# Letting two engines read one score slot in a gated attention kernel, with a re-tuned in-kernel scheduler

## Chip, cores, metric

One core of a Trainium2 chip. The time is the device time of one execution in microseconds (us); a lower time is better. "Span" is the part of it from the first to the last instruction of the profiled execution, about 2 us less than the time. Engines: PE is TensorE's matmul side, PEld its weight load, ACT is ScalarE, DVE is VectorE, POOL is GpSimd. PSUM is the memory that matmuls write, SBUF the working memory.

## The reference, cut

```python
# x: 1 x 2048 x 512, bf16; H = 32 heads of Dh = 16; W = 8, dil = 2
def _A_ref(x, wqkv, wo):                 # full attention
    q, k, v = qkv[0], qkv[1], qkv[2]
    scores = jnp.einsum("bhqd,bhkd->bhqk", q, k) * scale
    p = _softmax(scores, axis=-1)
    o = jnp.einsum("bhqk,bhkd->bhqd", p, v)
    return (...)(o, 0, 2, 1, 3).reshape(B, S, D) @ wo

def _B_ref(x, wqkv, wo):                 # 8 earlier positions, 2 apart
    ...
    attn = _softmax(logits, axis=-1)
    o = jnp.einsum("bhsw,bhswd->bhsd", attn, vg)
    return (...) @ wo

g = _sigmoid((x * gate_w).sum(-1, keepdims=True))
return g * _A_ref(x, A_wqkv, A_wo) + (1 - g) * _B_ref(x, B_wqkv, B_wo)
```

The full attention dominates: 32 heads x 2048 x 2048 scores, in this kernel 2048 tiles of 128 keys x 512 queries. Every score needs an exponential.

## The kernel before

The kernel is a Python program that *schedules itself*: `run()` simulates PE, ACT and DVE with its own cost figures, always moves the engine that is earliest in time, and emits the next instruction for it. So a constant or a condition that is changed in one place shifts the order of all that follows.

PSUM has two score slots `s_a` (three banks and two banks), one bank `acc` for the products with v, and two `flex` banks. PE writes three or two score tiles to a slot; ACT takes the exponential of the whole slot in one instruction. DVE takes single tiles from a flex bank with an integer trick: one pass out of PSUM gives int16 bit patterns (`yb`), three shifted copies follow, and the four of them, read as fp16, are each multiplied with v. That averages the trick's error, and costs PE four products instead of one.

```python
ACT_W = (3, 2)
NYB = 5            # buffers of DVE's batches
YB_ITEMS = 2       # tiles in a batch
MISC_SLACK = 10    # a flex bank is kept for other work due within so many tiles
BACKLOG = 3.0      # us of DVE work beyond which DVE is given no tile
WARM_WIN = 3.42
WARM_BAR = 3500

def exp_dve(slot_item):                  # DVE's first pass, PSUM to int16
    (b, kt, j), bt, i, bank = slot_item
    nc.vector.tensor_scalar(out=self.yb[bt["buf"]][:, 0, i*512:(i+1)*512], in0=bank[:],
                            scalar1=A, scalar2=..., op0=ALU.mult, op1=ALU.add)

def d_wanted(now):                       # may DVE have another tile?
    if min(fx_free) > now or p >= N - 24 or p % 64 >= D_LAST:
        return False
    ...
    if any(s.acq and s.due <= p + MISC_SLACK for s in ready):
        return False
    return max(0.0, t["DVE"] - now) + sum(s.cost for s in ready if s.eng == "DVE") < BACKLOG

# PE's turn, the next slot is free: scores for the slot, one more tile for DVE
# beside a slot of three, two beside a slot of two, if a flex bank is free
for _ in range(4 - ACT_W[si]):
    if d_wanted(now):
        ev.append(d_take(ACT_W[si] + 1, [d[0] for d in ev]))
n = min(ACT_W[si], N - p)
its = items[p:p + n]
p += n
end = emit_qk(ev, [(it, self.aslot[si][:, i, :]) for i, it in enumerate(its)], now)
slot_free[si] = INF
...
# ACT's turn: the whole slot; the slot is free when ACT is done
nc.scalar.activation(out=self.pt[pi[0]][pi[1]][:, 0:n * 512],
                     in_=self.aslot[si][:, 0:n, :].rearrange("p a b -> p (a b)"),
                     func=ACT.Exp, scale=SCALE)
slot_free[si] = now + c + 0.1

# local attention: q x shifted k in halves, five buffers; two matmuls to a half
nc.vector.tensor_tensor(out=pr[m % NPR][:], in0=bq[ct][:, HS * hf:HS * hf + HS],
                        in1=bk[ct][:, o:o + HS], op=ALU.mult)
for i in range(2):
    sc = 2 * (n % 2) + i
    nc.tensor.matmul(out=self.misc[32 * sc:32 * sc + 32, :], lhsT=self.Eh[:, n // 2, :],
                     rhs=pr[m % NPR][:, i * 512:(i + 1) * 512], ..., tile_position=(0, 32 * sc))

# local attention, later: its probabilities, broadcast by DMA (erb), times v
bs.append(self.dma(bc, 7.0, deps=...))   # 7.0 us: the latency that the scheduler assumes
nc.vector.tensor_tensor(out=st_["pw"][m % 2][:], in0=st_["erb"][m % 3][:], in1=win, op=ALU.mult)
```

Of the kernel before, what the change touches and what calls it, by code (L numbers as in the profile page):

```python
# [42 lines left out]
NYB = 5  # L43
NQM = 3
YB_ITEMS = 2
MISC_SLACK = 10
PART_US = 3.0
BACKLOG = 3.0
D_LAST = 58
# [664 lines left out]
class _Fast:  # L714
# [13 lines left out]
    def setup(self):  # L728
# [15 lines left out]
        self.oT = [c([P, S], BF16, name=f"oT{i}") for i in range(4)]  # L744
# [17 lines left out]
        self.flex = [p([P, 512], F32, name=f"flex{i}") for i in range(2)]  # L762
# [34 lines left out]
        ei = self.wk.tile([P, 16, 32], I32, name="ei", tag="t1")[:, 0:4, :]  # L797
        ef = self.wk.tile([P, 16, 32], F32, name="ef", tag="t1")[:, 0:4, :]
# [120 lines left out]
    def jobs(self):  # L919
# [75 lines left out]
        def gate_t():  # L995
            nc.vector.tensor_scalar(out=self.eg[:], in0=self.eg[:], scalar1=1e18, scalar2=None, op0=ALU.min)
            te = self.wk.tile([P, 16, 32], F32, name="t1", tag="t1")
            nc.vector.transpose(out=te[:].rearrange("p a b -> p (a b)"), in_=self.eg[:])
            gs = self.wk.tile([P, 16], F32, name="gs", tag="gs")
            nc.vector.tensor_scalar(out=gs[:], in0=te[:, :, 0], scalar1=1.0, scalar2=None, op0=ALU.add)  # L1000
            nc.vector.reciprocal(out=gs[:], in_=gs[:])
            for qc in range(NQC):
                for j in range(4):
                    nc.sync.dma_start(out=self.gA[32 * j:32 * j + 32, qc, :], in_=gs[32 * qc:32 * qc + 32, :])
# [8 lines left out]
    def jobs_b(self):  # L1013
# [4 lines left out]
        def b1_open():  # L1018
# [6 lines left out]
            for i in range(5):  # L1025
                pr[i] = BP["1"].tile([P, S // 2], BF16, name=f"prod{i}")
# [25 lines left out]
        NPR = len(range(5))  # L1052
        HS = S // 2
        for w in range(WIN):
            pd = []
            for n in range(8):
                m = 8 * w + n

                def prod(ct=n // 2, hf=n % 2, w=w, m=m):
                    o = PAD - DIL * w + HS * hf  # L1060
                    nc.vector.tensor_tensor(out=pr[m % NPR][:], in0=bq[ct][:, HS * hf:HS * hf + HS],  # L1061
                                            in1=bk[ct][:, o:o + HS], op=ALU.mult)
                s = Step("DVE", T_D2(HS), prod, deps=allp, rel=R1 + R1w * w + 5 * n, due=R1 + R1w * w + 60, cls=3)
                self.steps.append(s)
                pd.append(s)

            def lg(n, m):
                for i in range(2):
                    sc = 2 * (n % 2) + i
                    nc.tensor.matmul(out=self.misc[32 * sc:32 * sc + 32, :], lhsT=self.Eh[:, n // 2, :],  # L1070
                                     rhs=pr[m % NPR][:, i * 512:(i + 1) * 512], start=(n < 2), stop=(n >= 6),
                                     tile_position=(0, 32 * sc))

            def ex(w=w):
                nc.scalar.activation(out=self.er[:, w, :], in_=self.misc[:], func=ACT.Exp, scale=SCALE)  # L1075
                if w:
                    nc.gpsimd.memset(self.er[0:32, w, 0:DIL * w], 0.0)
            ch = self.chain([("PE", MM, lambda n=n, w=w: lg(n, 8 * w + n)) for n in range(8)] +
                            [("ACT", T_ACT(512), ex)], due=R1 + R1w * w + 70, deps=pd[:NPR])
            for n in range(8):  # L1080
                ch[n].deps.append(pd[n])
                m = 8 * w + n
                lgs.append(ch[n])
                if m >= NPR:
                    pd[n].deps.append(lgs[m - NPR])
                    if n >= NPR:
                        pd[n].cls = 0
# [9 lines left out]
        def den_ev():  # L1097
# [4 lines left out]
            st_["erb"] = [b2([P, 4, 512], BF16, name=f"erb{i}") for i in range(3)]  # L1102
# [9 lines left out]
        prev = den = ch[-1]  # L1112
# [27 lines left out]
        for sc in range(4):  # L1140
            for ct in range(4):
# [3 lines left out]
                for hf in range(2):  # L1145
                    m = 2 * i + hf

                    def bc(sc=sc, ct=ct, m=m, hf=hf):
                        for hl in range(8):
                            p = 32 * sc + 8 * ct + hl  # L1150
                            nc.sync.dma_start(  # L1151
                                out=st_["erb"][m % 3][16 * hl:16 * hl + 16, :, :].rearrange("p w s -> p (w s)"),
# [15 lines left out]
                for hf in range(2):  # L1168
                    m = 2 * i + hf

                    def prod(i=i, hf=hf, m=m):
# [3 lines left out]
                        nc.vector.tensor_tensor(out=st_["pw"][m % 2][:], in0=st_["erb"][m % 3][:], in1=win,  # L1175
# [22 lines left out]
        self.check_flag(self.guard + [den])  # L1198
# [87 lines left out]
    def run(self):  # L1286
        nc = self.nc
        NB = 32
        items = [(b, kt, j) for b in range(NB) for kt in range(NKT) for j in range(4)]
# [7 lines left out]
        slot_free = [SLOT_0] * na  # L1297
        nextslot = 0
# [10 lines left out]
        fx_free = [1.5, DVE_0]  # L1309
# [35 lines left out]
        def exp_dve(slot_item):  # L1345
            (b, kt, j), bt, i, bank = slot_item
            A = SCALE * math.log2(math.e) * 1024.0
            nc.vector.tensor_scalar(out=self.yb[bt["buf"]][:, 0, i * 512:(i + 1) * 512], in0=bank[:],  # L1348
                                    scalar1=A, scalar2=1024.0 * (15.0 + PW_S[0]), op0=ALU.mult, op1=ALU.add)

# [6 lines left out]
        def close_batch():  # L1357
# [4 lines left out]
            prev = bt["p1"][-1]  # L1362
            lasts = []
            for k in range(1, NP_):
                s = Step("DVE", T_D4(n), lambda k=k: piece(bt, k), deps=list(bt["p1"]), due=bt["due"], cls=2)
                self.steps.append(s)
                lasts.append(s)

            def done(end):
                for i, it in enumerate(bt["items"]):  # L1370
                    rhs = [self.yb[bt["buf"]][:, k, i * 512:(i + 1) * 512].bitcast(F16) for k in range(NP_)]
                    add_pv(it, rhs, end, ("y", bt))
                bt["refs"] = len(bt["items"])
            lasts[-1].on_done = done

        def add_pv(it, rhs, ready, src):
# [5 lines left out]
            q.insert(i, [b, kt, rhs, ready, src])  # L1382

        def emit_pv_one(j, now):
            b, kt, rhs, ready, src = pvq[j][0]
# [4 lines left out]
            r = rhs.pop(0)  # L1390
            last = False
            if not rhs:
                pvq[j].pop(0)
                jleft[(b, j)] -= 1
                last = jleft[(b, j)] == 0
                left[b] -= 1
                kind, ref = src
                if kind == "p":
                    pt_refs[ref] -= 1
                    if pt_refs[ref] == 0:  # L1400
                        pt_free[ref] = now + 0.45
                else:
                    ref["refs"] -= 1
                    if ref["refs"] == 0:
                        yb_free[ref["buf"]] = now + 0.45
# [8 lines left out]
        def norm_steps(b, now):  # L1414
# [3 lines left out]
            def n1():  # L1418
                h["t1"] = self.wk.tile([P, 16, 32], F32, name="t1", tag="t1")
                nc.vector.transpose(out=h["t1"][:].rearrange("p a b -> p (a b)"), in_=self.acc[:])  # L1420

            def n2():
                rc = self.wk.tile([P, 16], F32, name="rc", tag="rc")
                nc.vector.reciprocal(out=rc[:], in_=h["t1"][:, :, DH])
                nc.vector.tensor_tensor(out=rc[:], in0=rc[:], in1=self.gA[:, qc, :], op=ALU.mult)
                nc.vector.tensor_tensor(out=self.t2[(b // 2) % 2][:, :, 16 * par:16 * par + 16], in0=h["t1"][:, :, 0:DH],
                                        in1=rc[:].unsqueeze(2).to_broadcast([P, 16, DH]), op=ALU.mult)
# [7 lines left out]
            s2 = Step("DVE", 0.75, n2, deps=[s1, self.gate_done], due=64 * b + 40, cls=2)  # L1435
            self.steps += [s1, s2]
            if par == 1:
                s3 = Step("DVE", 0.62, n3, deps=[s2], due=64 * b + 40, cls=2)
# [21 lines left out]
        def take_step(s, eng, now):  # L1460
            if s.acq:
                s.chain["i"] = min(range(2), key=lambda i: fx_free[i])
# [27 lines left out]
        def d_wanted(now):  # L1490
            if min(fx_free) > now or p >= N - 24 or p % 64 >= D_LAST:
                return False
            if batch is None and min(yb_free) > now:
                return False
            ready = [s for s in self.steps if s.rel <= p and s.eng in ("PE", "DVE") and ready_time(s) <= now + 1.5]
            if any(s.acq and s.due <= p + MISC_SLACK for s in ready):
                return False
            return max(0.0, t["DVE"] - now) + sum(s.cost for s in ready if s.eng == "DVE") < BACKLOG

        def d_take(reach, taken):  # L1500
            nonlocal p, batch
            b = items[p][0]
            js = [it[2] for it in taken]
            win = [i for i in range(p, min(p + reach, 64 * (b + 1))) if items[i][2] not in js]
            x = min(win, key=lambda i: (dcount.get((b, items[i][2]), 0), i))
            it = items.pop(x)
            items.insert(p, it)
            p += 1
# [9 lines left out]
            fi = min(range(2), key=lambda i: fx_free[i])  # L1518
            fx_free[fi] = INF
            bank = self.flex[fi]  # L1520
            d0 = Step("X", 0, None)
            s = Step("DVE", T_D1(512), lambda: exp_dve((it, bt, n, bank)), deps=[d0], due=0, cls=1)

            def p1done(end):
                fx_free[fi] = end
# [8 lines left out]
        def emit_qk(dv, ac, now):  # L1534
            nonlocal mode
            for it, dst in [d[:2] for d in dv] + ac:
                b, kt, j = it
                ct, qc, par = geo(b)
                nc.tensor.matmul(out=dst, lhsT=self.kT[ct % 2][32 * j:32 * j + 32, kt * 128:(kt + 1) * 128],  # L1539
                                 rhs=self.qm[(4 * ct + qc) % NQM][par][32 * j:32 * j + 32, :],  # L1540
                                 start=True, stop=True, tile_position=(32 * j, 0))
            did_work(now, 128 * (len(dv) + len(ac)))
# [9 lines left out]
        while True:  # L1552
# [19 lines left out]
            if eng == "ACT":  # L1572
# [7 lines left out]
                elif aq:  # L1580
# [3 lines left out]
                    if start <= now:  # L1584
                        aq.pop(0)
                        n = len(its)
                        nc.scalar.activation(out=self.pt[pi[0]][pi[1]][:, 0:n * 512],  # L1587
# [152 lines left out]
```

## Time and profile before

| before | value | from |
|---|---|---|
| time, median of the first 5 runs | 797.59 us | the times |
| time, median of all 15 runs beside the changed kernel | 798.31 us (796.36 to 799.72) | the times |

Two more views are needed. First the groups by form for DVE and for the local attention's matmuls. The columns are line, engine, operation, out<-in, shapes, count, then busy us and mean ns of one, then idle time of the engine just before them and what ended it.

```profile
L1348 DVE TENSOR_SCALAR yb<-flex 128x512 int16<-128x512 f32 x371 | 246.3, 681 | 35.2 <-PE s_a L1539 27.5 <-PE flex L1539 6.6
...
L1354 DVE TENSOR_SCALAR yb<-yb 128x1024 int16<-128x1024 int16 x537 | 199.4, 418 | 1.3
...
L1354 DVE TENSOR_SCALAR yb<-yb 128x512 int16<-128x512 int16 x39 | 9.0, 286 | 0.0
...
L1070 PE MATMUL flex<-prod,Eh 128*32 128x512 bf16 x128 | 24.7, 387 | 0.1
```

Second, the one hole in the middle, in the timeline of all engines (start, duration, instruction, count; in brackets the idle time before it and what ended that).

```profile
476.05 1.23 DVE L1175 TENSOR_TENSOR pw<-erb,vc 128x2048 bf16<-128x2048 bf16 x1 [2.31 <-DMA erb<-er_dram]
477.19 0.71 DVE L1420 STREAM_TRANSPOSE t<-acc 128x512 f32<-128x512 f32 x1
...
477.96 0.62 PE L1407 MATMUL acc<-pt,vaug 128*32 128x512 bf16 x4 [2.34 <-DVE t L1420]
...
478.51 0.61 PE L1539 MATMUL s_a<-qm,kT 32*128 32x512 bf16 x2
...
479.15 1.02 ACT L1587 ACTIVATE pt<-s_a 128x1024 bf16<-128x1024 f32 x1 [2.27 <-PE s_a L1539]
```

Read it from the top: DVE stands 2.31 us before a DMA. Behind that product waits a transpose that clears `acc`, so PE stands 2.34 us; behind PE's products wait the next scores; so ACT stands 2.27 us. One late transfer passes through three engines, each of which does its work in order.

### The profile page before, as it was taken

The numbers are of one execution on the slowest core, as the hardware profiler recorded it, in microseconds if no ns is written. First come the engines' busy times: TensorE is split into PE (matmuls) and PEld (weight loads), VectorE is DVE, ScalarE is ACT, GpSimd is POOL, SyncE is SP. The second block draws the span as 40 slices with busy tenths as digits, with TensorE's granted clock in tenths as the row PEclk, the third lists the DMA queues.
The fourth block names the chain that finished last, engine by engine and source line by source line (L and its number), as shares of the span: only waits on it lengthen the run. The fifth ranks groups of instructions, "written<-read, shape, count | busy, mean of one in ns | idle before, by whom it ended". The sixth has DMA issues, their size and how long they took to land.

```text
span 797.9 us, 20303 instructions
## 1 busy us (share of the span) xinstructions
PE 735.4 (92%) x8438; PEld 241.9 (30%) x8438; DVE 684.9 (86%) x1447; ACT 767.7 (96%) x686; POOL 6.1 (1%) x25
## 2 busy tenths in 40 slices
PE   8999999999999888999988989989998999999995
PEld 4333333333322222222322222223322322332232
DVE  5789999896789999999999966998999988877861
ACT  4899999999999999999999998999999999999994
POOL 1000000000000000000000000000000000000000
PEclk9999999999999999999999998999999999999999
DMA  5110000000000000000000345312222221000001
GB/s 152 56 29 15 8 8 9 8 2 8 15 8 1 9 1 1 2 2 2 1 2 1 116 124 138 89 56 53 74 54 60 71 51 48 15 22 15 15 14 32
DMA packets 26070, 27.65 MB, mean 35 GB/s; under 512 B 16881, under 2 KB 21489, under 8 KB 25841
## 3 DMA queue, kind: packets, MB, share of 16 engines
q1 hardware_dynamic: 25120, 24.70, 11.5%
q8 instruction: 68, 1.11, 0.6%
q0 software_dynamic: 288, 1.05, 0.4%
q10 hardware_dynamic: 560, 0.52, 0.2%
q14 instruction: 34, 0.27, 0.1%
HBM read 23.07 MB, written 3.15 MB: 33 GB/s over the span
## 4 chain that ended last, share of the span: by engine, by line
ACT 53%; issue 18%; PE 18%; DVE 6%; SPq 3%; DMA 0%; DVEq 0%; ACTq 0%
ACT pt L1587 53%; PE acc L1407 5%; PE flex L823 5%; PE s_a L1539 4%; SPq L1151 3%; DVE yb L1348 2%; PE flex L1539 2%; DVE yb L1354 1%; DVE prod L1061 1%; ACT er L1075 1%; PE s_a L860 0%; DVE pw L1175 0%; PE s_a L823 0%; PE flex L887 0%; PE flex L1070 0%
## 5 line engine op out<-in xcount | busy, mean ns | idle before, releaser
L1587 ACT ACTIVATE pt<-s_a 128x1536 bf16<-128x1536 f32 (+1 forms) x671 | 761.9, 1365 | 11.9 <-PE s_a L1539 10.5
L1539 PE MATMUL s_a<-qm,kT 32*128 32x512 bf16 x1677 | 264.4, 384 | 44.3 <-ACT pt L1587 40.7
L1348 DVE TENSOR_SCALAR yb<-flex 128x512 int16<-128x512 f32 x371 | 246.3, 681 | 35.2 <-PE s_a L1539 27.5
L1407 PE MATMUL acc<-pt,vaug 128*32 128x512 bf16 x1677 | 254.0, 387 | 3.2 <-DVE t L1420 3.2
L1407 PE MATMUL acc<-yb,vaug 128*32 128x512 f16 x1484 | 212.6, 384 | 0.0
L1354 DVE TENSOR_SCALAR yb<-yb 128x1024 int16<-128x1024 int16 (+1 forms) x576 | 207.6, 409 | 1.3
L1539 PEld LDWEIGHTS <-kT 32*128 32x128 bf16 x2048 | 93.8, 91 | 322.6 <-issue 316.5
L1539 PE MATMUL flex<-qm,kT 32*128 32x512 bf16 x371 | 125.5, 383 | 2.7 <-DVE yb L1348 1.5
L1407 PEld LDWEIGHTS <-vaug 128*32 128x32 bf16 x3161 | 85.4, 95 | 134.6 <-issue 95.5
L823 PE MATMUL flex<-xT,ww 128*32 128x512 bf16 x1280 | 103.1, 384 | 2.0 <-DVE xT L866 0.5
L1175 DVE TENSOR_TENSOR pw<-erb,vc 128x2048 bf16<-128x2048 bf16 x32 | 39.0, 1219 | 8.7 <-DMA erb<-er_dram 7.5
L1061 DVE TENSOR_TENSOR prod<-bq,bk 128x1024 bf16<-128x1024 bf16 x64 | 42.0, 682 | 2.2 <-PE flex L1070 2.1
L823 PE MATMUL flex<-pw,ident 128*32 128x512 bf16 x512 | 42.0, 394 | 0.3 <-DVE yb L1348 0.2
L823 PEld LDWEIGHTS <-ww 128*32 128x32 bf16 x1280 | 26.7, 95 | 34.6 <-issue 26.4
L1420 DVE STREAM_TRANSPOSE t<-acc 128x512 f32<-128x512 f32 x32 | 22.6, 706 | 11.9 <-PE acc L1407 11.9
L1070 PE MATMUL flex<-prod,Eh 128*32 128x512 bf16 x128 | 24.7, 387 | 0.1
L849 DVE TENSOR_SCALAR qm<-flex,pmask 128x512 bf16<-128x512 f32 x31 | 22.7, 740 | 1.7 <-PE flex L823 1.7
L853 DVE TENSOR_REDUCE amx<-flex 128x1 f32<-128x512 f32 x32 | 21.8, 681 | 0.0
L1332 PE MATMUL acc<-wz 128*32 128x512 bf16 x160 | 20.5, 382 | 0.0
L823 PE MATMUL flex<-wAv,xT 128*32 128x128 bf16 (+1 forms) x512 | 18.3, 274 | 0.4 <-DVE vaug L842 0.4
L1190 DVE CAST oB<-flex 128x512 bf16<-128x512 f32 x16 | 11.0, 686 | 8.4 <-PE flex L823 8.4
L823 PE MATMUL flex<-woB,oB 128*32 128x512 bf16 x224 | 17.2, 382 | 0.0
(90 smaller groups left out, 231.9 us busy)
## 6 DMA issues: line engine op xcount, KB each, us to landing
erb<-er_dram SPq DMA_DIRECT2D x256, 64.0 KB, 2.3
out_dram<-ob SPq DMA_DIRECT2D x14, 128.0 KB, 1.7
x_in<-in_A_x_dram SPq DMA_DIRECT2D x3, 512.0 KB, 6.3
ww<-in_B_wqkv_dram SPq DMA_DIRECT2D x12, 128.0 KB, 2.5
ww<-in_A_wqkv_dram SPq DMA_DIRECT2D x8, 128.0 KB, 2.7
er_dram<-er SPq DMA_DIRECT2D x1, 1024.0 KB, 5.1
woA<-in_A_wo_dram POOLq DMA_DIRECT2D x1, 512.0 KB, 4.3
woB<-in_B_wo_dram POOLq DMA_DIRECT2D x1, 512.0 KB, 5.0
```

What stands on the lines that cost most here:

```text
L823: self.nc.tensor.matmul(out=out_ps[32 * c:32 * c + 32, 0:n], lhsT=lhsT_of(c), rhs=rhs, start=start, stop=stop, tile_position=(0, 32 * c))
L849: self.nc.vector.tensor_scalar(out=self.qm[(4 * ct + sc) % NQM][par][:], in0=self.misc[:], scalar1=self.pmask[:, par:par + 1], scalar2=Non ...
L1061: nc.vector.tensor_tensor(out=pr[m % NPR][:], in0=bq[ct][:, HS * hf:HS * hf + HS], in1=bk[ct][:, o:o + HS], op=ALU.mult)
L1070: nc.tensor.matmul(out=self.misc[32 * sc:32 * sc + 32, :], lhsT=self.Eh[:, n // 2, :], rhs=pr[m % NPR][:, i * 512:(i + 1) * 512], start=(n ...
L1151: nc.sync.dma_start(out=st_["erb"][m % 3][16 * hl:16 * hl + 16, :, :].rearrange("p w s -> p (w s)"), in_=st_["er_d"][p:p + 1, 2048 * hf:20 ...
L1175: nc.vector.tensor_tensor(out=st_["pw"][m % 2][:], in0=st_["erb"][m % 3][:], in1=win, op=ALU.mult)
L1348: nc.vector.tensor_scalar(out=self.yb[bt["buf"]][:, 0, i * 512:(i + 1) * 512], in0=bank[:], scalar1=A, scalar2=1024.0 * (15.0 + PW_S[0]), ...
L1354: nc.vector.tensor_scalar(out=y[:, k, 0:n], in0=y[:, 0, 0:n], scalar1=float(round(1024.0 * (PW_S[k] - PW_S[0]))), scalar2=None, op0=ALU.add)
L1407: nc.tensor.matmul(out=self.acc[32 * j:32 * j + 32, :], lhsT=v, rhs=r, start=first, stop=last, tile_position=(0, 32 * j))
L1420: nc.vector.transpose(out=h["t1"][:].rearrange("p a b -> p (a b)"), in_=self.acc[:])
L1539: nc.tensor.matmul(out=dst, lhsT=self.kT[ct % 2][32 * j:32 * j + 32, kt * 128:(kt + 1) * 128], rhs=self.qm[(4 * ct + qc) % NQM][par][32 * ...
L1587: nc.scalar.activation(out=self.pt[pi[0]][pi[1]][:, 0:n * 512], in_=self.aslot[si][:, 0:n, :].rearrange("p a b -> p (a b)"), func=ACT.Exp, ...
```

## The change

The intent: give DVE more tiles without more flex banks. When a full slot of three is about to be filled and DVE has less than `BACKLOG_S` of work, DVE takes the third tile *in the slot itself*, and ACT's instruction covers two banks instead of three. The two readers are declared independent of one another ("readers of different banks"); the next scores for the slot wait for both. To make room on DVE: batches of four tiles instead of two (fewer, wider copies), local products in whole tiles, normalisation for two heads at once. Space for that comes from laying two of the three `erb` tiles into `er`. Products with v are now released copy by copy, not after the last copy.

```diff
-NYB = 5
+NYB = 3
-YB_ITEMS = 2
-MISC_SLACK = 10
+NFLEX = 2
+YB_ITEMS = 4
+MISC_SLACK = 0
 BACKLOG = 3.0
+BACKLOG_S = 1.5
+SLOT_D = 3
@@ the scores of a slot @@
-                    its = items[p:p + n]
-                    p += n
-                    end = emit_qk(ev, [(it, self.aslot[si][:, i, :]) for i, it in enumerate(its)], now)
+                    slot_users[si] = 1
+                    slot_end[si] = 0.0
+                    if not ev and n == ACT_W[si] and n >= SLOT_D and (p + n - 1) // 64 == p // 64 and d_wanted(now, False):
+                        it = d_pick(n, [])
+                        items.insert(p + n - 1, it)
+                        n -= 1
+                        its = items[p:p + n]
+                        p += n + 1
+                        slot_users[si] = 2
+                        ev.append(d_add(it, self.aslot[si][:, n, :], lambda end, si=si: slot_done(si, end)))
+                    else:
+                        its = items[p:p + n]
+                        p += n
+                    end = emit_qk(ev, [(it, self.aslot[si][:, i, :]) for i, it in enumerate(its)], now,
+                                  si=si, share=slot_users[si] == 2)
@@ waits @@
+        def decouple(r):
+            ...
+            self.tc.declare_no_dep(a, d, reason="readers of different banks")
+            self.tc.declare_no_dep(d, a, reason="readers of different banks")
+            (DVE waits for its own score matmul, ACT for the two others)
+                if prev is not None and prev.get("share") and (share or it not in [d[0] for d in dv]):
+                    for k in ("act", "dve"):
+                        self.tc.add_manual_dep(raw(q), raw(prev[k]).name, info, reason="slot free")
@@ local attention @@
-            for i in range(5):
-                pr[i] = BP["1"].tile([P, S // 2], BF16, name=f"prod{i}")
+            for i in range(2):
+                pr[i] = BP["1"].tile([P, S], BF16, name=f"prod{i}")
+                for sc in range(4):
+                    nc.tensor.matmul(out=self.misc[32 * sc:32 * sc + 32, :], lhsT=self.Eh[:, ct, :],
+                                     rhs=pr[m % 2][:, sc * 512:(sc + 1) * 512], ..., tile_position=(0, 32 * sc))
-            st_["erb"] = [b2([P, 4, 512], BF16, name=f"erb{i}") for i in range(3)]
+            st_["erb"] = [self.er[:, 0:4, :], self.er[:, 4:8, :], b2([P, 4, 512], BF16, name="erb")[:]]
@@ cut: products released copy by copy, normalisation of two heads together, moved buffers @@
```

## The prediction

> **What bounds the kernel now.** I read the busy shares first, then the slices, then ScalarE's instruction forms, then who waits for whom, then stretches of time.
>
> ```profile
> PE 735.4 (92%) x8438; PEld 241.9 (30%) x8438; DVE 684.9 (86%) x1447; ACT 767.7 (96%) x686; POOL 6.1 (1%) x25
> ...
> DVE  5789999896789999999999966998999988877861
> ACT  4899999999999999999999998999999999999994
> ```
>
> ACT is busy 96% of 797.9 us, and its idle time sits in the first and last slice. PE (92%) and DVE (86%) are not far behind: whoever relieves ACT has little room elsewhere. The work is 2048 score tiles of 128x512 whose exponential is needed. ACT takes most of them, three or two to an instruction; DVE takes the rest by an integer trick (one pass out of PSUM, then three shifted copies, so four products with v instead of one).
>
> ```profile
> L1587 ACT ACTIVATE pt<-s_a 128x1536 bf16<-128x1536 f32 x335 | 527.5, 1575 | 4.9 <-PE s_a L1539 3.9 <-PE acc L1407 0.9
> L1587 ACT ACTIVATE pt<-s_a 128x1024 bf16<-128x1024 f32 x336 | 388.2, 1156 | 7.0 <-PE s_a L1539 6.6 <-PE acc L1407 0.2
> ```
>
> The groups of instructions by form, ACT alone. 335x3 + 336x2 = 1677 tiles, so DVE has 371. One more tile in an instruction costs 1575 - 1156 = 419 ns. Neighbours overlap: the page's union of both groups is 761.9 us (671 instructions), so beside the tiles each instruction costs (761.9 - 1677 x 0.419) / 671 = 0.088 us. ACT's idle before them is only 11.9 us.
>
> ```profile
> PE s_a L1539 <- ACT pt L1587: 40.7, 115, 1.0
> ACT pt L1587 <- PE s_a L1539: 10.5, 7, 4.4
> DVE pw L1175 <- DMA erb<-er_dram: 7.5, 5, 2.5
> ```
>
> The waits: PE waits for ACT to free a score slot 115 times, 40.7 us in all; the other way it is 7 times. So the path is ACT, not PE. Hence one tile taken from ACT is worth about 0.419 us of the end, as long as PE and DVE keep up.
>
> ```profile
> core 0: us, PE busy (x) PEld busy (x) DVE busy (x) ACT busy (x) POOL busy (x), PEclk, DMA share, GB/s
> 240.00:300.00 60.00, 53.01 (x508) 16.70 (x504) 59.22 (x128) 60.00 (x56) 0.09 (x1) 1.00 0.02 4
> 420.00:480.00 60.00, 53.60 (x542) 16.48 (x538) 51.00 (x103) 57.73 (x52) 0.00 (x0) 0.97 0.28 83
> 480.00:540.00 60.00, 55.23 (x638) 16.75 (x630) 51.13 (x103) 57.60 (x52) 0.00 (x0) 0.97 0.34 94
> 600.00:660.00 60.00, 55.90 (x629) 18.08 (x627) 55.64 (x125) 60.00 (x54) 0.00 (x0) 1.00 0.23 58
> ```
>
> The stretches: ACT is full (60.00 of 60) even where DVE is full too (59.22). The one hole in the middle is around 480 us, 2.3 + 2.4 us of ACT, with the granted clock at 0.97: there DVE stands before a broadcast DMA, PE behind DVE, ACT behind PE.
>
> **What the Trainium skill says.** "PSUM — Partial Sum Buffer", Specifications (TRN2): ScalarE and VectorE read PSUM side by side at full rate as long as they do not collide in a bank. The change lives on this: ACT and DVE will read different banks of one slot. The trace before agrees so far: DVE's 128x512 read of a flex bank takes 681 ns while ACT reads nearly always. "VectorE: DVE Perf Modes", The perf-mode tier table: a tensor_scalar on 16-bit SBUF data runs at 4x, 693 ns for 2048 elements. The trace has 418 ns for 1024 and 286 for 512, thus 132 ns per 512 and, extended, 682 for 2048: it agrees. "TensorE: Matmul & The Clock Gate", Part 1: after an idle window of some 3.4 us the array runs at half clock. The trace agrees: after DVE's stall near 477 us the groups of four matmuls come 0.43 us apart and not 0.22.
>
> **The change part by part.** A scheduler inside the kernel decides the order, so I counted instructions in the built program.
>
> (1) *ACT.* DVE may now take the third tile of a three-tile slot; that happens 64 times. Other settings change too, so the built program has 275 ACT instructions of 1536 and 404 of 1024: 825 + 808 = 1633 tiles, 44 fewer, in 679 instructions, 8 more. Cost: 1633 x 0.419 + 679 x 0.088 = 744.0 against 761.9: **-17.9 us**, on the path. By stages, in blocks of 64 tiles as DVE's order has them: DVE gets +19 tiles in the first nine blocks, +6 in the next eight, +12 and +7 after; so the gain is spread, and smallest where DVE was full.
>
> (2) *Start.* ACT stands for about 4.4 us near 22 us until the second chunk of keys exists. Two of the 44 tiles come off before that, and there ACT would only wait longer: **+0.8 us**.
>
> (3) *DVE.* First passes 415 instead of 371 at 246.3/371 = 0.664: +29.2. Copies: now mostly four tiles wide; 207.6 us before are 1113 tile-widths x 0.132 plus 576 x 0.105; after, 1245 widths and 348 instructions give 164.3 + 36.5 = 200.8: -6.8. The 64 half products (42.0) become 32 whole ones of the shape of pw (39.0 for 32): -3.0. Normalisation done for two heads at once: 26.8 us of small operations become about 18.6: -8.2. Sum +11 us: 696 of some 780, 89%. Off the path, but no longer with much room.
>
> (4) *PE.* Four products instead of one for each moved tile: +176 acc matmuls from DVE's tiles, -44 from ACT's, -16 fillers. They run four at a time in different column groups; counted so, the built program has 916 groups into acc against 918, so they fill gaps in groups. Score rounds rise from 693 to 717: 24 x about 0.32 us (score matmul to next matmul in the timeline) = +8 us. PE waits 40.7 us for ACT today, so it fits, with less left.
>
> (5) *Coupling.* After a shared round the next scores in that slot wait for ACT and DVE both. In the built program neither reader waits for the other of the same round. DVE's read needs 0.68 us plus its queue (the scheduler allows 1.5 us of backlog). ACT needs the slot back after its other slot (0.93) and this one (0.93), and has a further 0.93 before it starves, less about 0.5 for the scores. So DVE is late only now and then. I put 64 x 0.05 = **+3 us**, chosen, not derived.
>
> (6) *The stage near 480 us.* The broadcast tiles now lie in er's own space, still three buffers, same DMAs. But the first pw products stand among more exponentials: in DVE's order, the first eight span 47 rows instead of 27. They ask the DMAs for less at once. Of ACT's 4.7 us lost there, and some 2 us elsewhere, I take **-4 us**; new waits of this kind, from a schedule that differs everywhere, I put at **+1 us**.
>
> Sum: 797.6 - 17.9 + 0.8 + 3 - 4 + 1 = 780.5; the end-to-end cadence of full ACT stretches (about 1.34 and 0.92 us) makes (1) 18.2, and I round down to **780**.
>
> **The rivals.** *A: the wait moves to DVE.* DVE is in order, runs about 9% longer than the scheduler's own cost figures (0.664 against 0.608 for a first pass), and now holds a slot that ACT needs. If each of the 64 shared rounds loses 0.3 us, 19 us go and the time is about 797. For it: DVE is at 95 to 99% from 240 to 420 us. Against: only 9 of the 64 shared rounds stand in those blocks, and before the change PE hardly ever waits for DVE's first pass (1.5 us in all) though it already shares flex banks with it. *B: PE becomes the bound*, with more score rounds, fewer fillers and shorter ACT rounds; a cold stretch of 3.4 us costs ACT about a microsecond or two. Five more of them would give 787. For it: 92% busy. Against: the 40.7 us of waiting for ACT. *C: the DMA hole near 480 us and the other middle waits vanish wholly* and the coupling costs nothing: 797.6 - 17.1 - 6.5 = 774.
>
> **Range and chances.** The ACT term is counted and sure to about 1 us; what is open is ACT's lost time in the middle, 6 to 7 us today, which may become 1 (774) or 13 (787). The middle is 780, and the line for 2% is near 781.8, so it is close: predicted **780.0**, range **773.0 to 787.0**, faster by over 2% **0.6**, within 2% **0.39**, slower **0.01**.
>
> **What would show each step right or wrong.** ACT's exponentials: 679, union near 744 us, means still 1575 and 1156 (a longer mean says that two readers of one slot disturb each other, and that the skill's sentence does not hold). DVE first passes on s_a: 64 at 681 ns. DVE busy 690 to 705, PE 740 to 748. "PE s_a waits for DVE yb" in the waits: under 5 us if (5) holds, over 15 if rival A does; it would stand beside new ACT waits for PE. Near 480 us ACT idle under 3 us if (6) holds. PE's wait for ACT shrinks from 40.7 to some 25 to 35. The prediction is wrong if ACT's idle before its exponentials rises above 18 us (from 11.9), or if the clock falls in more stretches than now.

## The result, and the profile after

| | before | after |
|---|---|---|
| time, median (range, runs) | 798.31 us (796.36 to 799.72, 15) | 779.5 us (776.23 to 783.34, 8) |
| ratio, 95% interval | | 0.9762 [0.9744, 0.9781] |
| tiles by ACT / DVE (of these in a shared slot) | 1677 / 371 (0) | 1633 / 415 (64) |
| union of ACT's exponentials | 761.9 us | 743.7 us |
| ACT idle just before them | 11.9 us | 7.6 us |
| PE busy / DVE busy | 735.4 / 684.9 us | 723.7 / 702.0 us |

A ratio is the mean time of one kernel's fast runs over that of the other's in the same rounds, so it is not quite the ratio of the medians quoted. The result is faster, by 18.8 us in the medians.

The two *profiled* executions differ by more, 23.0 us of span (797.9 to 774.9): that of before was 2.0 us over its median (in time), with a mean granted clock of 0.989, and that of after 2.7 us under, with 0.998. The ten executions of the changed kernel whose clock is known go from 774.4 us of span at 0.997 to 781.5 at 0.986, some 0.6 us for each 0.001 of clock. What follows about the traces concerns these two executions.

Busy shares and slices of the changed kernel:

```profile
PE 723.7 (93%) x8554; PEld 232.4 (30%) x8554; DVE 702.0 (91%) x1186; ACT 749.6 (97%) x694; POOL 5.5 (1%) x25
...
DVE  5998999989899999999999999999999998878971
ACT  4999999999999999999999999999999999999994
```

ACT has no slice below 9 between the first and the last, and DVE's dent of two sixes is gone. Groups by form, ACT, then DVE, then the local matmuls:

```profile
L1654 ACT ACTIVATE pt<-s_a 128x1024 bf16<-128x1024 f32 x404 | 435.0, 1141 | 5.3 <-PE s_a L1597 5.2
...
L1654 ACT ACTIVATE pt<-s_a 128x1536 bf16<-128x1536 f32 x275 | 431.1, 1568 | 2.3 <-PE s_a L1597 1.3 <-PE acc L1432 0.8
...
L1351 DVE TENSOR_SCALAR yb<-flex 128x512 int16<-128x512 f32 x351 | 232.7, 681 | 26.1 <-PE s_a L1597 17.4 <-PE flex L1597 7.3
...
L1375 DVE TENSOR_SCALAR yb<-yb 128x2048 int16<-128x2048 int16 x273 | 178.2, 683 | 0.6
...
L1351 DVE TENSOR_SCALAR yb<-s_a 128x512 int16<-128x512 f32 x64 | 43.8, 684 | 6.2 <-PE s_a L1597 5.8
...
L1071 PE MATMUL flex<-prod,Eh 128*32 128x512 bf16 x128 | 14.1, 384 | 0.0
```

Sixty three-tile instructions have become 68 two-tile ones. DVE's read of a bank in a shared slot takes 684 ns, of a flex bank 681. If ACT's instructions are paired with DVE's reads round by round, the two reads overlap in time in 62 of the 64 rounds, and ACT's two-tile instructions still follow one another at 917 ns, as in the trace before. So the two readers do not disturb each other. The same 128 local matmuls now fill 14.1 us and not 24.7. The waits (who waits for whom; us in all, times, longest):

```profile
PE s_a L1597 <- ACT pt L1654: 34.5, 103, 1.0
...
PEld L1597 <- ACT pt L1654: 21.7, 47, 0.8
...
ACT pt L1654 <- PE s_a L1597: 6.5, 5, 4.8
...
PEld L1597 <- DVE yb L1351: 0.4, 1, 0.4
```

PE still waits for ACT, ACT for PE only five times, of which one is the start (4.8 us). The wait that the change could have brought, scores of a slot waiting for DVE, was seen once, 0.4 us. Part of it could hide where ACT released later than DVE; then it cost nothing: in the same pairing DVE was done with its bank before ACT in 58 of the 64 rounds, and over 0.5 us later in three. The stretches, in the columns of the stretch view shown in the prediction:

```profile
240.00:300.00 60.00, 54.67 (x541) 17.12 (x543) 59.40 (x90) 60.00 (x57) 0.58 (x3) 1.00 0.01 4
420.00:480.00 60.00, 57.39 (x641) 17.59 (x640) 58.11 (x99) 59.49 (x56) 0.00 (x0) 1.00 0.36 98
480.00:540.00 60.00, 57.76 (x696) 17.42 (x694) 55.00 (x95) 59.70 (x57) 0.00 (x0) 1.00 0.23 63
600.00:660.00 60.00, 57.82 (x706) 17.50 (x703) 53.49 (x99) 59.63 (x56) 0.00 (x0) 1.00 0.25 61
```

From 420 to 540 us ACT's idle time is 0.5 + 0.3 = 0.8 us; it was 2.3 + 2.4 = 4.7.

So the 23.0 us between the traces are: ACT's exponentials 18.2, ACT's idle time before them 4.3, the rest 0.5.

### The profile page after: what moved, and what is told of

The parts are those of the page before. It is cut to its first block, busy times and chain, and to the rows that moved or that the text cites.

```text
span 774.9 us, 20388 instructions
## 1 busy us (share of the span) xinstructions
PE 723.7 (93%) x8554; PEld 232.4 (30%) x8554; DVE 702.0 (91%) x1186; ACT 749.6 (97%) x694; POOL 5.5 (1%) x25
## 4 chain that ended last, share of the span: by engine, by line
ACT 58%; PE 20%; issue 19%; DVE 2%; ACTq 0%; DVEq 0%
ACT pt L1654 57%; PE flex L827 6%; PE acc L1432 5%; PE s_a L1597 5%; PE flex L1597 2%; ACT er L1076 1%; PE s_a L864 0%; PE s_a L827 0%; DVE yb L1351 0%; PE flex L891 0%; DVE prod L1063 0%; PE s_a L868 0%; DVE ob L1265 0%; DVE vaug L846 0%; PE acc L1335 0%
## 5 line engine op out<-in xcount | busy, mean ns | idle before, releaser
L1654 ACT ACTIVATE pt<-s_a 128x1024 bf16<-128x1024 f32 (+1 forms) x679 | 743.7, 1314 | 7.6 <-PE s_a L1597 6.5
L1597 PE MATMUL s_a<-qm,kT 32*128 32x512 bf16 x1697 | 265.9, 382 | 39.2 <-ACT pt L1654 34.5
L1351 DVE TENSOR_SCALAR yb<-flex 128x512 int16<-128x512 f32 x351 | 232.7, 681 | 26.1 <-PE s_a L1597 17.4
L1432 PE MATMUL acc<-yb,vaug 128*32 128x512 f16 x1660 | 238.7, 383 | 0.0
L1375 DVE TENSOR_SCALAR yb<-yb 128x2048 int16<-128x2048 int16 (+3 forms) x348 | 204.9, 627 | 0.7
L1597 PE MATMUL flex<-qm,kT 32*128 32x512 bf16 x351 | 120.8, 383 | 1.5 <-DVE vaug L846 0.3
L1432 PEld LDWEIGHTS <-vaug 128*32 128x32 bf16 x3293 | 78.0, 95 | 129.9 <-issue 102.0
L1351 DVE TENSOR_SCALAR yb<-s_a 128x512 int16<-128x512 f32 x64 | 43.8, 684 | 6.2 <-PE s_a L1597 5.8
L1063 DVE TENSOR_TENSOR prod<-bq,bk 128x2048 bf16<-128x2048 bf16 x32 | 38.3, 1217 | 0.2 <-PE flex L1071 0.2
L1444 DVE STREAM_TRANSPOSE t<-acc 128x512 f32<-128x512 f32 x32 | 22.7, 708 | 11.8 <-PE acc L1432 11.6
L1175 DVE TENSOR_TENSOR pw<-er,vc 128x2048 bf16<-128x2048 bf16 x22 | 26.8, 1218 | 0.4 <-issue 0.4
L857 DVE TENSOR_REDUCE amx<-flex 128x1 f32<-128x512 f32 x32 | 21.7, 681 | 0.0
L1335 PE MATMUL acc<-wz 128*32 128x512 bf16 x144 | 17.9, 381 | 0.0
L827 PE MATMUL flex<-woA,oT 128*32 128x512 bf16 x224 | 17.0, 384 | 0.0
```

What stands on the lines that cost most here:

```text
L827: self.nc.tensor.matmul(out=out_ps[32 * c:32 * c + 32, 0:n], lhsT=lhsT_of(c), rhs=rhs, start=start, stop=stop, tile_position=(0, 32 * c))
L857: self.nc.vector.tensor_reduce(out=self.amx[:, row, ct, sc:sc + 1], in_=self.misc[:], axis=AX.X, op=ALU.max, apply_absolute_value=True)
L1063: nc.vector.tensor_tensor(out=pr[m % 2][:], in0=bq[ct][:], in1=bk[ct][:, o:o + S], op=ALU.mult)
L1335: nc.tensor.matmul(out=self.acc[32 * j:32 * j + 32, :], lhsT=self.wz[:, 0:32], rhs=self.wz[:], start=False, stop=False, tile_position=(0, ...
L1351: ins = nc.vector.tensor_scalar(out=self.yb[bt["buf"]][:, 0, i * 512:(i + 1) * 512], in0=bank[:], scalar1=A, scalar2=1024.0 * (15.0 + PW_S ...
L1375: nc.vector.tensor_scalar(out=y[:, k, 0:n], in0=y[:, 0, 0:n], scalar1=float(round(1024.0 * (PW_S[k] - PW_S[0]))), scalar2=None, op0=ALU.add)
```

## The experiments

All twelve gave correct results. The table has them all; "ACT work" is the prediction's count, 0.419 us per tile and 0.088 per instruction. ACT idle and PE's wait for DVE's first pass are from the profiled execution. The runs were taken in sets on different chips; the kernel before, run beside each set, had medians of 797.3 to 799.5 us, so the ratio is the fairer comparison between sets.

| run | tiles shared | DVE tiles | ACT work | time, median us (runs) | ratio to before [95%] | ACT idle | PE waits for first pass |
|---|---|---|---|---|---|---|---|
| before | 0 | 371 | 761.7 | 798.31 (15) | 1 | 11.9 | 1.7 |
| after | 64 | 415 | 744.0 | 779.5 (8) | 0.9762 [0.9744, 0.9781] | 7.6 | 0.7 |
| e1_noshare | 0 | 384 | 755.8 | 796.57 (12) | 0.9968 [0.9941, 0.9995] | 10.4 | 2.6 |
| e2_backlog_s3 | 154 | 446 | 733.1 | 792.52 (4) | 0.9917 [0.9884, 0.9949] | 26.3 | 8.0 |
| e3_slot2 | 123 | 449 | 730.6 | 786.55 (4) | 0.9860 [0.9821, 0.9899] | 23.8 | 5.9 |
| e4_before_dma11 | 0 | 373 | 760.8 | 793.96 (4) | 0.9932 [0.9911, 0.9952] | 7.5 | 2.0 |
| e5_noshare_dma11 | 0 | 376 | 759.4 | 790.49 (20) | 0.9924 [0.9903, 0.9944] | 10.4 | 3.1 |
| e6_batches_of_two | 48 | 404 | 748.4 | 788.19 (4) | 0.9895 [0.9838, 0.9953] | 10.7 | 3.1 |
| e7_backlog_s2 | 101 | 428 | 739.4 | 781.35 (4) | 0.9804 [0.9776, 0.9832] | 15.5 | 4.4 |
| e8_dma11_backlog4 | 71 | 427 | 738.8 | 780.76 (4) | 0.9782 [0.9752, 0.9812] | 14.4 | 2.2 |
| e9_longer_hold_shared | 64 | 415 | 744.0 | 804.13 (17) | 1.0068 [1.0049, 1.0087] | 26.9 | 18.5 |
| e10_same_load_on_flex | 64 | 415 | 744.0 | 797.43 (20) | 0.9986 [0.9973, 0.9999] | 22.1 | 21.9 |
| e11_more_fillers | 76 | 425 | 739.9 | 777.69 (4) | 0.9738 [0.9706, 0.9770] | 10.5 | 2.2 |
| e12_misc_slack_10 | 96 | 419 | 743.3 | 782.85 (5) | 0.9794 [0.9771, 0.9816] | 13.0 | 5.4 |

**e1_noshare: the change without the sharing.**

```diff
-SLOT_D = 3
+SLOT_D = 4
```

> The changed kernel with the sharing of a three-tile slot switched off (a slot must have 4 tiles before DVE may take one, and none has). All else of the change stays. In the built program ACT has 1664 tiles in 666 instructions, so 1664 x 0.419 + 666 x 0.088 = 755.8 us of exponentials against 744.0. Theory (ACT is the path, a tile is worth 0.419 us): 779.5 + 11.8 = 791 us, ACT idle before its exponentials near that of the changed kernel (7.6 us). Rival (the gain comes from the wider batches, the finer product order and the missing hole near 480 us, and sharing only trades one wait for another): 783 us or less.

Measured: ratio 0.9968, median 796.57 against the 791 that I expected. Two things were missed. The hole is still there, and larger. Its stretches (same columns):

```profile
420.00:480.00 60.00, 55.52 (x567) 16.92 (x566) 51.19 (x85) 55.30 (x49) 0.00 (x0) 0.97 0.29 89
480.00:540.00 60.00, 53.09 (x621) 16.79 (x622) 51.84 (x85) 58.89 (x54) 0.00 (x0) 1.00 0.37 96
```

ACT loses 4.7 + 1.1 us there, and DVE's products again wait for the broadcast DMAs. And the mean clock of its twelve runs was 0.987 against 0.9935 for the changed kernel. So everything in the diff except the sharing is worth 2 to 3 us here; the sharing makes the other 16.4 (0.0206 of 798). The difference in ACT work is only 755.8 - 744.0 = 11.8; the rest goes with the hole and the clock, which this run does not tell apart.

**e2_backlog_s3, e7_backlog_s2 and e3_slot2: more sharing.**

```diff
-BACKLOG_S = 1.5
+BACKLOG_S = 3.0    # e2;  2.0 in e7
```
```diff
-SLOT_D = 3
+SLOT_D = 2         # e3: also the second tile of the two-bank slot
```

> The changed kernel with the backlog that DVE may have when it takes a tile out of a shared slot raised from 1.5 to 3.0 us: 154 shared rounds instead of 64, DVE 446 tiles instead of 415, ACT work 733.1 us instead of 744.0. Theory while ACT stays the path and the slot comes back in time: 779.5 - 10.9 = 768.6 us. Rival A (DVE holds the slot): DVE gets 31 tiles x about 1.15 us = 36 us more, 738 us busy, and the slot waits for it; waits of PE for DVE yb above 10 us and a time of 776 us or more.

> Between the change (backlog 1.5 us, 64 shared rounds, 779.5 us) and backlog 3.0 us (154 rounds, 792.5 us): backlog 2.0 us, 101 rounds, ACT work 739.4 us. If ACT alone were the path: 779.5 - 4.6 = 775 us. From the other two runs: with 154 rounds ACT's idle before its exponentials was about 25 us instead of 7.6, which is 0.2 us per extra round; so 37 more rounds cost about 7 us and give back the 4.6: 781 to 783 us. Waits of PE for DVE's first pass between the 0.4 us of the change and the 7.8 us of backlog 3.0.

> The changed kernel with sharing allowed in the two-tile slot as well: 70 + 53 shared rounds, DVE 449 tiles, ACT work 730.6 us in 689 instructions. Theory while ACT stays the path: 779.5 - 13.4 = 766 us. Rival A: DVE about 39 us busier (741 us), and a two-tile slot whose ACT part takes only about 0.5 us comes back late; then 774 us or more with new ACT waits for PE behind DVE.

Measured: each takes more from ACT and none is faster; e2 and e3 are clearly slower than the change, e7 came as forecast (781 to 783), but its interval overlaps the change's. ACT work 744.0, 739.4, 733.1 for thresholds of 1.5, 2.0, 3.0 us; ACT idle 7.6, 15.5, 26.3; time 779.5, 781.4, 792.5. The waits of e2:

```profile
ACT pt L1654 <- PE s_a L1597: 16.5, 28, 4.0
...
ACT pt L1654 <- PE acc L1432: 8.6, 7, 2.2
...
PEld L1597 <- DVE yb L1351: 4.6, 11, 0.8
...
PE s_a L1597 <- DVE yb L1351: 1.9, 5, 0.7
```

At 3.0 us something like rival A appears: PE waits for DVE's first pass 8.0 us (under the 10 that the forecast named), and ACT waits for PE's scores 28 times where it had been five. What costs most here is not told apart. DVE is also busy 29.7 us more (731.7 against 702.0); at the 0.4 us per us that e10 below measures, this alone would be an estimated 12 of the 24 us lost (13.0 in the medians and 10.9 of ACT work saved). So the threshold keeps the change clear of a loss, but whether the held slot or DVE's load makes it is open.

e3 shows another limit. Its groups by form:

```profile
L1654 ACT ACTIVATE pt<-s_a 128x1536 bf16<-128x1536 f32 x274 | 412.9, 1507 | 11.3 <-PE s_a L1597 8.2 <-PE acc L1432 1.8
...
L1654 ACT ACTIVATE pt<-s_a 128x512 bf16<-128x512 f32 x53 | 34.3, 648 | 5.7 <-PE s_a L1597 5.7
```

In that trace one tile takes ACT 0.49 us end to end, and of the 53 instructions that follow such a one, 49 end at least 0.16 us later than the full cadence allows: 18 of them by 0.16 to 0.18 us, the others by up to 0.97; the median of all is 0.28. In the 0.49 us the *other* slot must be refilled, and it is not. So I estimate the round trip of a slot, from ACT's end through the score matmuls to ACT's next instruction, at 0.49 + 0.16 = 0.65 us or more; an ACT instruction shorter than that starves the next one. The sharing of the change leaves 0.92 us (two tiles), which is long enough.

**e4_before_dma11 and e5_noshare_dma11: the hole by itself.** The scheduler's assumed latency of the broadcast DMA, in the kernel before (e4) and in the change without sharing (e5):

```diff
-                    bs.append(self.dma(bc, 7.0, ...
+                    bs.append(self.dma(bc, 11.0, ...
```

> The kernel before with one number of its scheduler changed: the latency it assumes for a broadcast of er from 7 to 11 us, so that it spreads the first pw products (order in DVE: first eight over 75 rows instead of 27). ACT work 760.8 against 761.7 us, thus nearly unchanged. Theory (the hole near 480 us is DVE before a DMA, PE behind DVE, ACT behind PE): the ACT idle of 4.7 us between 420 and 540 us falls under 1.5 us and the time by 3 to 5 us, ratio about 0.995. Rival (the hole is due to something else in that stage, as flex banks or the cold clock alone): time within 1 us of the kernel before, hole still there.

> The changed kernel without sharing, and with the broadcast latency that the scheduler assumes at 11 us instead of 7. Without sharing alone the time was 796.6 us and ACT stood 6.2 us between 474 and 492 us. ACT work is 759.4 us, 3.6 more than without sharing alone. Theory (the hole is one cause and the tiles are the other): hole under 1.5 us, time 796.6 + 3.6 - 5.5 = about 794 us, and its runs closer together than the 792 to 803 us of the one with the hole. Rival (the loss without sharing has another source than the broadcasts): 797 us or more, hole still there.

Measured: e4 has ratio 0.9932, median 793.96, as expected. Its stretches:

```profile
420.00:480.00 60.00, 54.96 (x541) 17.01 (x536) 56.83 (x120) 60.00 (x54) 0.00 (x0) 1.00 0.26 76
480.00:540.00 60.00, 57.63 (x669) 17.98 (x668) 48.93 (x95) 59.90 (x54) 0.00 (x0) 1.00 0.31 86
```

ACT is full in both, and DVE's wait for the broadcast falls from 7.5 to 0.2 us:

```profile
DVE pw L1175 <- PE flex L823: 8.3, 6, 2.4
...
DVE pw L1175 <- DMA erb<-er_dram: 0.2, 1, 0.2
```

DVE now waits for PE instead (8.3 us, before: 0.8), and ACT does not feel it. So one constant in the old kernel is worth about 5.4 us (0.0068 of 798), with no sharing. e5 has ratio 0.9924, 790.49, better than the expected 794. Fifteen of its twenty runs have a span of 786.4 to 789.3 at a clock of 0.994 or more, five have 793.5 to 796.9 at 0.980 to 0.985; the profile fell on one of the five. With the hole treated, the change without sharing is thus no better than the old kernel with the hole treated. Against e5, the sharing is worth 0.0162 of 798, 12.9 us, for 15.4 us of ACT work.

**e6_batches_of_two: the change with the old batches.**

```diff
-NYB = 3
-YB_ITEMS = 4
+NYB = 5
+YB_ITEMS = 2
```

> The changed kernel, sharing on, with DVE's batches as before: two tiles in five buffers instead of four in three. The 348 copies become 636 narrower ones, which cost about 19 us more of DVE by 132 ns per 512 plus 105 ns each for the same tiles; the scheduler then gives DVE 404 tiles instead of 415, 48 shared. ACT work 748.4 us. Theory: only the work counts, 779.5 + 4.4 = 784 us. Rival (wider batches were the main thing of the change): 790 us or more.

Measured: 788.19, interval 0.9838 to 0.9953: inconclusive between the two forecasts. Two of its runs have spans of 782 and 783 us at clock 0.997, two have 790 at 0.984. At like clock it is thus about 7 us slower than the change (774.4 to 775.6 at 0.995 to 0.998), of which 748.4 - 744.0 = 4.4 is ACT work: DVE, busy 709.9 us, gets 11 tiles fewer. That points to wide batches as what pays for part of the sharing, but on four runs only.

**e8_dma11_backlog4: can the idle time that is left be won?**

```diff
-BACKLOG = 3.0
+BACKLOG = 4.0
@@ and the assumed latency 7.0 -> 11.0, as in e5 @@
```

> An attempt at a better version: the change, with the broadcast latency assumed at 11 us, and the backlog for tiles that go through a flex bank (not a shared slot) at 4.0 instead of 3.0 us. DVE 427 tiles, 71 of them shared, ACT work 738.8 us, 5.2 less than the change. Theory (a flex bank holds up no slot of ACT's, so longer DVE queues are cheap there): 779.5 - 5.2 = 774 us. Rival (DVE, at 91%, is full, and the longer queue makes PE wait for copies): 779 us or more, with new waits of PE acc for DVE yb.

Measured: 780.76, no better than the change; the expected 774 was missed. ACT work fell by 5.2 us, to 738.8, ACT's idle time rose by 6.8, to 14.4. In this order ACT stands 1.4 + 4.7 us in the two stretches from 420 to 540 us, some of it behind PE's products into `acc` (1.85 and 1.35 us) with hardly any wait of DVE for a DMA (0.9 us there). The hole is thus not cured by any one constant: where the local attention's products meet the score rounds, each order has its own waits.

**e9_longer_hold_shared and e10_same_load_on_flex: what a longer hold of a slot costs.** Both add 64 useless DVE operations of 0.68 us (128x512, f32), in an otherwise unchanged order. In e9 each stands just before a first pass on a shared slot, so that the slot is held so much longer; in e10 each stands before every fifth first pass on a flex bank, the same load elsewhere.

```diff
+            if id(bt["items"][i]) in self.shared:                     # e9
+            if id(bt["items"][i]) not in self.shared: (every fifth)   # e10
+                z = self.wz[:].bitcast(F32).unsqueeze(1).to_broadcast([P, 2, 256])
+                nc.vector.tensor_tensor(out=self.dum[:]..., in0=z, in1=z, op=ALU.mult)
```

> The changed kernel, instruction for instruction, plus one useless VectorE operation of about 0.69 us (a 128x512 float product of zeros into a tile that nobody reads) just before each of the 64 reads of a shared slot: DVE gets 44 us more and holds each shared slot 0.69 us longer. Theory (DVE is off the path, slots come back in time with little to spare): a part of the 64 x 0.69 is absorbed; +5 to +20 us, seen as waits of PE for DVE's first pass on s_a. Rival A as it was put (the wait has already moved to DVE in the changed kernel): the whole 44 us, about 823 us.

> The control: the same 64 useless operations, before every fifth read of a flex bank and not of a shared slot. DVE gets the same 44 us. If only the holding of a slot costs, this stays within 5 us of 779.5; if DVE's total load is what costs (91% busy, 97% with this), it costs as much as the other one. My guess is +2 to +8 us, less than half of the other.

Measured: e9 804.13, e10 797.43, so +24.6 and +17.9 us over the change. Both came out above the forecast: +5 to +20 for e9, +2 to +8 for e10. The waits of e9:

```profile
ACT pt L1658 <- PE s_a L1601: 23.9, 37, 5.4
...
PE s_a L1601 <- DVE yb L1355: 12.1, 31, 0.9
...
PE flex L1601 <- DVE yb L1355: 4.6, 14, 0.7
```

and of e10:

```profile
ACT pt L1660 <- PE s_a L1603: 19.1, 35, 6.7
...
PE flex L1603 <- DVE yb L1357: 13.3, 34, 0.8
```

The wait moves from `s_a` to `flex`, and ACT suffers nearly as much. ACT's idle time is not all of the loss. The groups of e10:

```profile
L1660 ACT ACTIVATE pt<-s_a 128x1024 bf16<-128x1024 f32 (+1 forms) x679 | 749.4, 1238 | 22.1 <-PE s_a L1603 19.1 <-PE acc L1438 0.8
```

The same 679 instructions fill 749.4 us, 749.7 in e9, and not 743.7: one that starts late loses its overlap with the one before (a two-tile one takes 1.023 us alone and 0.917 in a full stretch). This adds about 6 us to the 14.5 that the idle column of the table shows.

44 us of extra load on DVE cost 17.9 us even away from the shared slots, 0.4 us for each, although DVE was at 91%. Both runs put the load just before a read out of PSUM; a third, with the same load before the copies, was not made, so it is not shown that the load costs this wherever it stands. The longer hold of a slot adds 6.7 us, 0.10 us a round; but e9's runs also had a lower mean clock than e10's (0.987 against 0.993), which at 0.6 us per 0.001 would be about half of that. Whether the lower clock came of the stalls or by itself stays open. My idea that only a *shared* read sits on the path was wrong: a flex read stands in the same in-order queue of PE.

**e11_more_fillers: the clock.** The scheduler adds useless matmuls when PE was idle; a higher bar makes it add 447 instead of 144.

```diff
-WARM_BAR = 3500
+WARM_BAR = 4300
```

> The changed kernel with a higher bar for calling PE cold (4300 instead of 3500), so 447 filler matmuls instead of 144. ACT work 739.9 us (the schedule shifts a little: DVE 425 tiles, 76 shared). Theory on the scatter of runs (776 to 783 us at granted clocks of 0.998 to 0.986: stretches at half clock delay score rounds): the runs come at a clock of 0.996 or more and lie within 3 us of each other, at 779.5 - 4.1 - 2 = 773 us. Rival (fillers stand in PE's order and delay the scores; or the scatter has another cause): 780 us or more, or the same scatter.

Measured: 777.69, ratio 0.9738, clocks 0.995 to 0.999 in four runs that lie within 2.2 us. The forecast of 773 us was missed; that the runs come closer together held. It is the best point of all, but its interval overlaps that of the change, and its order differs too (425 DVE tiles, ACT work 739.9). So a better kernel than the change is not shown.

**e12_misc_slack_10: the old reserve of flex banks.**

```diff
-MISC_SLACK = 0
+MISC_SLACK = 10
```

> The changed kernel with MISC_SLACK back at 10 as before (DVE leaves the flex banks earlier to the other work). DVE has 419 tiles instead of 415 and ACT work is 743.3 instead of 744.0, so nearly the same work; but 96 of the tiles come from shared slots instead of 64. This tells apart what makes more sharing cost in e2, e3 and e7. If each shared round beyond 64 costs ACT 0.2 to 0.26 us by holding the slot: 32 x 0.23 - 0.7 = +7 us, about 786. If it is DVE's load (17.9 us for 44 us more in e10, so 0.4 us per us; here 4 tiles x 1.15 us): +1 us, about 781.

Measured: 782.85, between the two forecasts. With the reserve, flex banks are refused more often, so 96 tiles go by the shared slot instead of 64, at nearly the same ACT work (743.3). ACT's idle time rises by 5.4 us and the ratio by 0.0032, 2.6 us in 32 more shared rounds: again near 0.1 us a round, if all of it is put down to the sharing; the intervals of the two ratios overlap, so it can also be nothing.

## Why the prediction was right, and where it was not

The time (780.0 against 779.5), the class and the range held. Step by step:

1. **ACT, -17.9 us: right.** 679 instructions, union 743.7, so -18.2. The means are 1141 and 1568 ns, not longer than 1156 and 1575. A mean shrinks when an instruction starts late, so the better sign is the end-to-end cadence of full stretches, 917 and 1343 ns in both traces. So the sentence of the Trainium skill ("PSUM — Partial Sum Buffer", Specifications (TRN2)) on ScalarE and VectorE side by side held here for two banks of one slot: 684 against 681 ns.
2. **Start, +0.8: a wash.** The wait near 21 us was 4.37 us, after another of 1.07, and became 4.81. Against e4, whose start is the old one without the 1.07, it is +0.7. The old trace had an earlier wait that the prediction did not count.
3. **DVE 696: nearly.** 702.0, inside the 690 to 705 given. First passes 232.7 + 43.8 = 276.5 (predicted 275.5), copies 204.9 (200.8), whole products 38.3 (39.0), normalisation 20.0 (18.6). The copy of four tiles took 683 ns, as extended from the narrower ones.
4. **PE 740 to 748: wrong.** It fell to 723.7. The step counted what was added, and took the local attention's matmuls as unchanged because their number, 128, is. In halves two column groups work at a time, in whole products four: 24.7 us became 14.1, a gain of 10.6 that the diff showed and the step did not count. The rest of the gap lies partly in the old trace, whose hole ran at half clock. PE's wait for ACT, 25 to 35 predicted, was 34.5, with 21.7 more booked on the weight loads (none in the trace before), so it is not shown that it shrank. PE was off the path, so the miss left the time alone.
5. **Coupling, +3: mis-sized in the traced run.** One wait of 0.4 us. Nothing hides in lost overlap either: ACT's exponentials fill 3.9 us more than the full cadence would need, before as after. The longer hold of e9 and the extra rounds of e12 give about 0.1 us a round when provoked.
6. **The hole, -4: size right, reason only half.** 4.7 us became 0.8, 3.9 less, and e4 shows by itself that the hole is worth about 5.4 us of time. Not the new place of the broadcast tiles did it: e1 has that too, and keeps the hole. The order has changed. From the first to the eighth of DVE's products pw it takes 28.6 us in the old trace, 26.7 in e1, 34.0 in the changed kernel (425.23 to 459.22) and 52.2 in e4 (461.98 to 514.17); the two short ones wait for DMAs, the two long ones do not. But the spread alone does not decide: e11 has 26.1 us and waits 0.2 us for DMAs, e8 has 40.2 and waits 2.0. In the old trace the queue's broadcasts for one product come about 4.0 us apart (first issues at 449.25 for the first product and 481.46 for the ninth), and DVE, held back by them, gets through one product every 4.1 us. Its lead is only 2.5 us: so long after its broadcast has landed does the first product start. The lead is 5.2 us in the changed kernel, 4.8 in e11, 7.4 in e4, but 3.4 in e1. So it looks like lead and spread together, against the rate of the broadcasts; no run varies them singly. That the spread widens was in the prediction; that it would not without the sharing (e1) was not. **New waits +1:** what is left of ACT's idle time in the middle is small in the traced run; a typical run is some 2.7 us longer, at a lower clock, for which the sum had no term.

**The skill's sentence on the clock: half seen.** The prediction cites "TensorE: Matmul & The Clock Gate", Part 1, for half clock after an idle window of some 3.4 us and says that the trace agrees. The half clock is there, from 476.8 us on for 6.8 us. The idle window is not: in the 3.4 us before, PE was busy for 1.6 us, and its longest idle time there is 2.34 us, of which 1.2 had passed.

That the sum came within 0.5 us is in part luck. From trace to trace the gain is 23.0 us of span and not 18.8 (the medians), because the execution traced before lay above its median and the one after below; the sum has no term for that scatter, and step 5, too large, happens to offset it. Rival A (64 x 0.3 us) did not appear in the changed kernel: one wait of 0.4 us. That it is because few shared rounds stand where DVE is full, as the prediction argued, was not tested; e2, with a higher threshold, goes part of the way towards it. Rival B did not appear: PE has less work than before. Rival C, 774, was not reached: the fastest execution took 776.2 us.

Left open: how far the scatter of single runs is the clock alone, since e11 changes the order too; what sets the clock of an execution; how much the wide batches are worth; whether load on DVE costs as much when it does not stand before a read out of PSUM; and what sets the hole, lead or spread.

## What to carry to other kernels

To relieve the bound engine, count its work before and after in the built program, then look for the threshold at which the helper becomes the path: here ACT's exponentials fell by 0.41 us for each tile moved at a backlog of 1.5 us, and at 3.0 most of the gain was lost again. A helper at 91% that works in order is no free reserve: of 44 us put on DVE before its reads out of PSUM, 18 came out at the end before flex reads and 25 before shared ones. When a diff changes how an operation is cut up, count the parallel groups of each matmul and not their number.

## What the Trainium skill lacked or had wrong

- "PSUM — Partial Sum Buffer" gives the rules of banks but no round trip of a bank between TensorE and its reader. Here, from ScalarE's end through the score matmuls to ScalarE's next instruction, it is an estimated 0.65 us or more (e3: 0.49 us that an instruction of one tile covers, and the 0.16 us or more by which the next one is late), which bounds the shortest useful instruction on two slots.
- "ScalarE: Activation LUTs", What ACT_TABLE_LOAD costs, has 186 ns + 0.833 ns per element (scale and bias as constants) and an overlap of about 93 ns back to back, thus, estimated from these, 946 ns for 1024 columns and 1373 for 1536. Full stretches here run at 917 and 1343 ns end to end, in both traces: 29 and 30 ns less for each. Alone the instructions take 1023 and 1451 ns, so the overlap is 106 to 108 ns.
- "TensorE: Matmul & The Clock Gate", Part 1, puts half clock after at least one idle window of about 3.4 us. Here it came without one: between 30 and 760 us, ten of the traces hold twelve half-clock stretches (3.4 to 20.5 us), and in the 3.4 us before each PE was busy for 1.6 to 3.1 us (ends of matmuls are modelled) with no idle time over 1.3 us up to that moment. What does set it off stays open. It matters for a change of 2%: the same program took spans of 774.4 to 781.5 us, 0.9%, at mean clocks of 0.997 to 0.986.
- No page tells what extra load on an in-order engine near full load costs the engines that wait for it: 64 operations of 0.68 us, added to DVE at 91%, cost 17.9 us before flex reads and 24.6 us before shared ones.
